# Agents innermost in `signed_weights`, with the second sets written by ScalarE and by the eviction

## The chip, the cores and the metric

The kernel is a Bass and Tile program on one core of one Trainium2 chip. The metric is the device time of one execution in microseconds, on that core, as the median of several runs. Engines are named as in the profile: PE (TensorE matmul), PEld (TensorE weight load), DVE (VectorE), ACT (ScalarE), POOL (GpSimd) and SP (the engine that issues DMAs).

## The reference, cut to what matters

```python
# attention through 49 agents: B, N, C = 4, 10048, 128
a2k = sm(agents, k)                 # softmax of scale * agents @ k.T
agent_v = a2k @ v                   # 49 x 128 per batch
x = (sm(q, agents) @ agent_v).reshape(B * N, C)
# mixture of experts: 4 groups of 4 experts, F = 1024
g_idx = argmax(x @ w_group, 1)                  # and its softmax weight g_w
e_idx = argmax(x @ w_expert[g_idx], 1)          # and its softmax weight e_w
out = g_w * e_w * (relu(x @ w1[g, e]) @ w2[g, e])   # one expert for each row
```

Each row of x is a convex mixture of 49 agent rows of its batch. So for one expert, x @ w1 is a mixture of the 49 rows of agent_v @ w1, and a hidden unit whose 49 entries all have one sign is linear (or zero) for every row.

## The kernel before, in words

The four batches run in the order 1, 2, 0, 3 of the input, called batch 0 to 3 here. For each batch there is work of four sorts: keys and values to agent_v (`agents_of`), queries to the softmax rows and the routing (`queries_of`, `routing`, `output_weight`), the weights of the batch's most frequent expert (`weights_in`), and the tiles of that expert (`tiles`): per tile of 512 rows three units of `first` (products with the small weights into a PSUM bank `ph`, eviction `hh` by ACT, remainder `hl` by DVE) and `second` (into `po`), and three `check` products into `pv`, whose largest violation ACT gathers (`spare`). `second` runs three units behind `first` (LAG = 3). Rows of the third batch that go to other experts are done by `taken`, which prepares the weights of two more experts (`prepare_kept`).

**What sets the order.** All of this is written as generators, six streams (m tiles, a agents, q queries, w weights, s stores, g gathers). Everything for batch 0 up to its weights stands in a hand-written list (ORDER); after that the string PLAN has one letter for a step of a stream (z is one idle matmul that nobody reads), and each `yield` ends a step. Every engine runs its instructions in exactly that program order. So an instruction put on another engine takes the place, in that engine's queue, at which its step stands in PLAN.

**The edited function.** `signed_weights` makes one expert's weights for `first`, and runs six times: for batch 0, 1, 2, for two kept experts, for batch 3. These are calls 1 to 6. Its stages:

- Ordering. Eight matmuls (w1f as weights, the 49 agents moving) give the coefficients, `ps`, 128 x (8 blocks of hidden units x 49 agents). ACT evicts them as `mt` (fp32) and `mh` (fp16, in the trace mth). On DVE: the sum `ss` and the sign s16 of each hidden unit, `ms` = mh times the sign, the deviation `dv` (it lives in the tile of ml), times `peak` and its minimum; the square of mt and its sum; a key for each unit; `below` and `cntf` count keys under 32 levels; two PE products and a scan give each unit a position `pos`. `peak` is a bound for each agent of a batch, made in `peaks` (three times, for batches 1 to 3) and used here.
- One-hots. `hot` (8 comparisons of 512 positions on DVE) sorts the hidden units by position.
- Second copies. The weight operand of a product has 98 columns, the 49 agents twice, since `first` multiplies by 49 high parts and 49 low parts. So mh, ml = mt - mh (mtl), mt and mv (mtv) each have two equal sets of 49.
- Products on PE, all reading the one-hots: mh and ml (8 each, 384 columns), `whl` (24, 256 columns: w2 sorted, its high and low part), mt with w2f (8 products in fp32, two records each in the trace, for what lies beyond the first 384 positions), mv with `hot` (8, 128 columns), and then mv with a second set of one-hots (8, 512 columns).

Before, each of the four tiles is laid out as [P, 2, NA, FB]: set, agent, block, with the block innermost. `twice` takes all 98 columns of one block, so it reads every eighth element. The PSUM bank has the block outermost, so its evictions and the reductions over agents (`rearrange("p a k -> p k a")`) step by eight elements too. The second set is in every case a DVE `tensor_copy`, right behind what makes the first.

**PSUM.** Pool `psa` has five banks with one tag, "at". All of the products above, the transposes of `turn`, the units `ph` and the checks `pv` take their bank there in program order. `ps2` has two banks for `po`, and one bank is for the idle matmuls. Tiles of pool `rt` (mt, mth, mtl, mtv, hot, ...) have one buffer.

Of the kernel before, what the change touches and what calls it, by code (L numbers as in the profile page):

```python
# [10 lines left out]
F32 = mybir.dt.float32  # L11
F16 = mybir.dt.float16
# [3 lines left out]
AF = mybir.ActivationFunctionType  # L16
ALU = mybir.AluOpType
AX = mybir.AxisListType
# [4 lines left out]
P = 128  # L23
# [3 lines left out]
NA = 49  # L27
# [3 lines left out]
FB = F // P  # L31
# [169 lines left out]
def build(ctx, tc, qT, kT, v, agT, wr, w1, w2, cpk, out):  # L201
    nc = tc.nc
    pe, vec, act, pool, sync = [Pinned(x) for x in (nc.tensor, nc.vector, nc.scalar, nc.gpsimd, nc.sync)]
# [6 lines left out]
    const = ctx.enter_context(tc.tile_pool(name="const", bufs=1))  # L210
# [3 lines left out]
    rt = ctx.enter_context(tc.tile_pool(name="rt", bufs=1))  # L214
# [9 lines left out]
    def bank(b=1):  # L224

        if alone[0] and b == 0:
            turns[0] += 1
            k = turns[0] % 8
            if k in (1, 4):
                return ps2.tile([P, TQ, C], F32, name="po").rearrange("p a c -> p (a c)")  # L230
        return psa.tile([P, 512], F32, name="at", tag="at")
# [5 lines left out]
    def cc(name):  # L237
        o, w = CCOL[name]
        return cp[:, o:o + w]
# [11 lines left out]
    pool.memset(flags, 0.0)  # L251
    within = const.tile([P, 2, MOSTH + 1], F32, name="within")
    pool.memset(within, 0.0)
    peak = const.tile([P, NA, FB], F16, name="peak")
    pool.memset(peak, 0.25)
    two = const.tile([P, NA], F32, name="two")
    vec.tensor_add(out=two, in0=identf[:, 0:NA], in1=identf[:, HALF:HALF + NA])
# [198 lines left out]
    def agents_of(b):  # L456

        state[b] = {}
        st = state[b]
        n = len(chunks)  # L460
        yield from skewed(n, lambda ci: load_only("k", b, ci), lambda ci: key_load(b, ci), lambda ci: key_scores(b, ci))
        yield from key_max(b)
        yield from skewed(n, lambda ci: value_load(b, ci), lambda ci: value_exp(b, ci), lambda ci: value_products(b, ci))
        acc = st["acc"]
        sides = [slice(x, x + NA) for x in (0, HALF)]
        av = rt.tile([P, C + 1], F32, name="av2")
        pool.memset(av[HALF // 2:HALF], 0.0)
        act.activation(av[sides[0]], acc[sides[0], 0:C + 1], AF.Copy)
        yield FINE
        vec.tensor_copy(out=av[sides[1]], in_=acc[sides[1], 0:C + 1])  # L470
        yield
        ps = bank(b)
        both = slice(0, SIDES)
        pe.matmul(ps[:, 0:NA], av[both, C:C + 1].broadcast_to([SIDES, P]), two[both], start=True, stop=True)
        pe.matmul(ps[:, NA:2 * NA], av[both, 0:C], two[both], start=True, stop=True)
        yield
        za = sm.tile([P, NA], F32, name="za2")
        vec.tensor_scalar(out=za, in0=ps[:, 0:NA], scalar1=1e-9, scalar2=None, op0=ALU.add)
        vec.reciprocal(out=za, in_=za)
        avT = sm.tile([P, NA], F32, name="avT")  # L480
        vec.tensor_mul(out=avT, in0=ps[:, NA:2 * NA], in1=za)
        yield
        yield from agents_scaled(b, avT)

    def front(b, early, order, later):
# [34 lines left out]
        for x in order:  # L520
# [87 lines left out]
            elif o == "J":  # L608
                parted["q", b, c] = split_load("q", b, c)
            elif o == "z":  # L610
                busy(c)
            elif o == "i":
                busy(c, psT[:, 384:512])
            elif o == "A":
                psT = main_soon(b, early, a0, se, busy)
                alone[0] = False
            elif o == "D":
                scaled = scaled or coarse(agents_scaled(b, psT[:, 0:NA]))
                for _ in range(c):
                    next(scaled, None)  # L620
            elif o == "U":
                uf = early.tile([P, P], F32, name="uf")
                pin(sync.dma_start(out=uf, in_=cpk[:, CUSED:CUSED + P]))
                pool.tensor_copy(out=upper, in_=uf)
            elif o == "W":
                weights = signed_weights(b, wbuf[b % 2], state[b].pop("wf"))
                counted = coarse(weights)
                for _ in range(c):
                    next(counted)
                pinned(())  # L630
            elif o == "F":
                all_of(logits_of(b, 0))
            elif o == "R":
                all_of(routing(b, *RANGES[0]))
            elif o == "n":
                for _ in range(c):
                    next(later)
# [395 lines left out]
    def peaks(b):  # L1033

        st = state[b]
        pm = rt.tile([P, NT, NA], F16, name="pm", tag="hot")
        for i in range(0, NT, 20):
            t = slice(i, min(i + 20, NT))
            vec.tensor_mul(out=pm[:, t], in0=rows[:, t, 0:NA], in1=st["inv"][:, t].unsqueeze(2).broadcast_to([P, t.stop - i, NA]))
            yield  # L1040
        vec.tensor_max(out=pm[:, 0:39], in0=pm[:, 0:39], in1=pm[:, 40:79])
        yield FINE
        for n in (20, 10, 5):
            vec.tensor_max(out=pm[:, 0:n], in0=pm[:, 0:n], in1=pm[:, n:2 * n])
        px = sm.tile([P, NA], F32, name="px")
        vec.tensor_reduce(out=px, in_=pm[:, 0:5].rearrange("p t a -> p a t"), axis=AX.X, op=ALU.max)
        yield
        ps = bank(b)
        pe.transpose(ps[0:NA, 0:P], px, identf)
        yield  # L1050
        ma = sm.tile([NA, 1], F32, name="ma")
        vec.tensor_reduce(out=ma, in_=ps[0:NA, 0:P], axis=AX.X, op=ALU.max)
        yield
        ps = bank(b)
        pe.matmul(ps[:, 0:NA], ma.broadcast_to([NA, P]), identf[0:NA, 0:NA], start=True, stop=True)
        yield
        vec.tensor_copy(out=peak, in_=ps[:, 0:NA].unsqueeze(2).broadcast_to([P, NA, FB]))
        yield

    def signed_weights(b, to, wf):  # L1060
# [2 lines left out]
        w1f, w2f = wf  # L1063
        wb = to.bitcast(F16)
        f32 = lambda n, name: rt.tile([P, n], F32, name=name)
        of_k = lambda a: a.unsqueeze(1).broadcast_to([P, NA, FB])
        twice = lambda a, k: a.rearrange("p i a k -> p (i a) k")[:, :, k]
        ps = bank(b)
        for k in range(FB):
            pe.matmul(ps[:, k * NA:(k + 1) * NA], w1f[:, k * P:(k + 1) * P], st["at"][:, 0:NA], start=True, stop=True)  # L1070
        yield
        psk = ps[:, 0:FB * NA].rearrange("p (k a) -> p k a", a=NA)
        psa_ = psk.rearrange("p k a -> p a k")
        mt2 = rt.tile([P, 2, NA, FB], F32, name="mt")
        mh2, ml2, mv2 = [rt.tile([P, 2, NA, FB], F16, name=name) for name in ("mth", "mtl", "mtv")]
        mt, mh, ml, mv = [x[:, 0] for x in (mt2, mh2, ml2, mv2)]
        act.activation(mt, psa_, AF.Copy)
        yield FINE
        act.activation(mh, psa_, AF.Copy)
        yield FINE  # L1080
        ss, qq, mu, mn, va, key, pl, sg = [f32(FB, "f" + name) for name in ("ss", "qq", "mu", "mn", "va", "key", "pl", "sg")]
        vec.tensor_reduce(out=ss, in_=psk, axis=AX.X, op=ALU.add)
# [6 lines left out]
        vec.scalar_tensor_tensor(out=mu, in0=ss, scalar=1.0 / NA, in1=s16, op0=ALU.mult, op1=ALU.mult)  # L1089
        yield  # L1090
        dv = ml
        sq = rt.tile([P, NA, FB], F32, name="sq", tag="big")
        ms = mv
        vec.tensor_mul(out=ms, in0=mh, in1=of_k(s16))
        yield FINE
        vec.tensor_sub(out=dv, in0=ms, in1=of_k(mu))
        yield FINE
        vec.tensor_mul(out=dv, in0=dv, in1=peak)
        yield FINE
        vec.tensor_reduce(out=mn, in_=dv.rearrange("p a k -> p k a"), axis=AX.X, op=ALU.min)  # L1100
        yield
        vec.tensor_mul(out=sq, in0=mt, in1=mt)
        yield FINE
        vec.tensor_reduce(out=qq, in_=sq.rearrange("p a k -> p k a"), axis=AX.X, op=ALU.add)
        yield FINE
        vec.tensor_add(out=mn, in0=mn, in1=mu)
        yield FINE
# [16 lines left out]
                          in1=cc("level").unsqueeze(2).broadcast_to([P, MOSTH, FB]), op=ALU.is_lt)  # L1124
        yield FINE
        cnt = rt.tile([P, MOSTH], F16, name="cntf")
        with nc.allow_low_precision("counts of at most 8"):
            vec.tensor_reduce(out=cnt, in_=below, axis=AX.X, op=ALU.add)
        yield
        ps = bank(b)  # L1130
# [4 lines left out]
                          in1=cc("most").unsqueeze(2).broadcast_to([P, 2, MOSTH]), op=ALU.is_le)  # L1135
# [6 lines left out]
                       in1=sel.unsqueeze(2).broadcast_to([P, 2, 2, MOSTH]))  # L1142
# [33 lines left out]
        for k in range(FB):  # L1176
            vec.tensor_scalar(out=hot[:, k], in0=wide, scalar1=pos[:, k:k + 1], scalar2=None, op0=ALU.is_equal)
            if k % 4 == 3:
                yield
        vec.tensor_copy(out=mh2[:, 1], in_=mh)  # L1180
        yield FINE
        vec.tensor_sub(out=ml, in0=mt, in1=mh)
        yield FINE
        vec.tensor_copy(out=ml2[:, 1], in_=ml)
        yield FINE
        whl = rt.tile([P, FB, 2, C], F16, name="whl", tag="big")
        act.activation(whl[:, :, 0], w2f, AF.Copy, scale=W2S)
# [3 lines left out]
        for src, to_ in ((mh2, 0), (ml2, WLO)):  # L1191
            ps = bank(b)
# [5 lines left out]
        yield FINE  # L1198
        vec.tensor_mul(out=mt, in0=mt, in1=of_k(sg))
        yield FINE  # L1200
        vec.tensor_copy(out=mt2[:, 1], in_=mt)
        yield FINE
        vec.tensor_reduce(out=qq, in_=mh.rearrange("p a k -> p k a"), axis=AX.X, op=ALU.max, apply_absolute_value=True)
        yield FINE
        vec.tensor_scalar(out=qq, in0=qq, scalar1=2.0 ** -9, scalar2=2.0 ** -23, op0=ALU.mult, op1=ALU.add)
        yield FINE
        vec.tensor_sub(out=mv, in0=ms, in1=of_k(qq))
        yield FINE
        vec.tensor_copy(out=mv2[:, 1], in_=mv)
        yield  # L1210
        for j0 in range(0, FULL, 2):
            n = min(2, FULL - j0)
            ps = bank(b)
# [6 lines left out]
        ps = bank(b)  # L1220
# [9 lines left out]
        for h, (f0, f1) in enumerate(((EX, TS), (0, TS))):  # L1230
# [6 lines left out]
            ps = bank(b)  # L1237
# [20 lines left out]
    def weights_in(b):  # L1258

        yield from output_weight(b)  # L1260
        yield from peaks(b)
        yield from signed_weights(b, wbuf[b % 2], state[b].pop("wf"))
# [560 lines left out]
    def one_by_one(*gens):  # L1823

        for gen in gens:
            yield from gen
            yield "end"
# [4 lines left out]
        a=one_by_one(*[agents_of(b) for b in later_ones]),  # L1832
# [35 lines left out]
```

## Time and profile before

| | |
|---|---|
| median of 3 runs | 816.7 us (815.06 to 817.57) |
| the profiled execution: its time | 810.57 us |
| its span | 808.8 us |
| granted TensorE clock, mean | 0.975 |
| PE busy | 744.7 us, 92% |
| PEld busy | 559.9 us, 69% |
| DVE busy | 644.3 us, 80% |
| ACT busy | 502.3 us, 62% |
| POOL busy | 379.3 us, 47% |
| SP | issues DMAs only, not counted as busy |

The span is from the first to the last record of the profile; the execution's time has 1.8 us more. PEld runs beside PE, so their times overlap. One helper records every operation, so all rows of the trace name one line, L185; the tile names (out<-in) tell what an instruction is.

### The profile page before, as it was taken

The page shows a single profiled execution, that of the slowest core. Times are in us where ns is not written, and L with a number is a line of the kernel's source. Part 1 is how long each engine was busy: PE and PEld are TensorE (multiplying, and loading weights), DVE is VectorE, ACT ScalarE, POOL GpSimd, SP SyncE. Part 2 cuts the span into 40 slices and gives each one's busy share as a digit, 9 for nine tenths or more (in the row PEclk, how much of TensorE's full clock was granted, in tenths as well). Part 3 has the DMA queues.
Part 4 walks back from the last instruction along what each step waited for, and adds up shares of the span by engine and source line. Part 5 has one row for each costly group of instructions (what it writes and reads, how often), then busy time and mean ns, then how long its engine had stood idle before and what let it go on. Part 6 is the DMA issues. An engine that isn't in the chain of part 4 may idle for free.

```text
span 808.8 us, 23174 instructions
## 1 busy us (share of the span) xinstructions
PE 744.7 (92%) x9350; PEld 559.9 (69%) x9350; DVE 644.3 (80%) x1455; ACT 502.3 (62%) x1075; POOL 379.3 (47%) x619
## 2 busy tenths in 40 slices
PE   7888999999998899999979998899999998999994
PEld 6664767767765577888647755677787675977773
DVE  6869978976889886777997899958968987876663
ACT  5543577759955444899555323447988775457772
POOL 4235574129941521688385216843663226542220
PEclk9979999999999999999998999999999998999997
DMA  9844143497623737443366040175402373112211
GB/s 321 318 158 156 38 147 118 122 319 205 178 67 142 230 100 248 123 136 94 98 253 191 7 156 18 16 210 152 147 15 71 109 247 88 58 43 63 67 54 53
DMA packets 66276, 107.93 MB, mean 133 GB/s; under 512 B 5223, under 2 KB 46136, under 8 KB 65776
## 3 DMA queue, kind: packets, MB, share of 16 engines
q1 hardware_dynamic: 64816, 104.54, 40.1%
q0 software_dynamic: 1344, 1.82, 1.0%
q8 instruction: 75, 1.23, 0.6%
q14 instruction: 41, 0.34, 0.2%
HBM read 73.97 MB, written 32.47 MB: 132 GB/s over the span
## 4 chain that ended last, share of the span: by engine, by line
PE 52%; DVE 21%; ACT 5%; issue 3%; DMA 2%; POOL 1%; another core or an unknown queue 1%; SPq 0%; ACTq 0%; POOLq 0%; DVEq 0%
PE po L185 17%; PE at L185 17%; PE ph L185 10%; PE pv L185 5%; DVE hl L185 4%; PE idle L185 3%; DVE pm L185 2%; DMA vf<-v 1%; DVE oh L185 1%; ACT hh L185 1%; ACT xh L185 1%; DMA w1f<-w 1%; DVE rd L185 1%; DVE rx L185 1%; POOL xl L185 1%
## 5 line engine op out<-in xcount | busy, mean ns | idle before, releaser
L185 POOL TENSOR_TENSOR xl<-xf,xh 128x256 f16<-128x256 f32 (+2 forms) x280 | 194.0, 725 | 147.7 <-ACT xh L185 134.3
L185 DVE SCALAR_TENSOR_TENSOR hl<-ph,hh 128x512 f16<-128x512 f32 (+1 forms) x256 | 172.8, 678 | 75.1 <-ACT hh L185 70.9
L185 PE MATMUL po<-wbuf,hh 128*128 128x128 f16 x1896 | 185.2, 219 | 0.3 <-issue 0.3
L185 ACT ACTIVATE hh<-ph 128x512 f16<-128x512 f32 (+1 forms) x256 | 151.4, 592 | 53.5 <-PE ph L185 47.7
L185 PEld LDWEIGHTS <-hh 128*128 128x128 f16 x2022 | 161.2, 98 | 32.1 <-issue 1.1
L185 PE MATMUL po<-wbuf,hl 128*128 128x128 f16 x948 | 171.2, 219 | 0.0
L185 PE MATMUL ph<-et,wbuf 98*128 98x512 f16 x480 | 141.9, 377 | 9.9 <-DVE hl L185 4.6
L185 ACT ACTIVATE spare<-pv 128x512 bf16<-128x512 f32 (+1 forms) x158 | 93.4, 591 | 81.1 <-PE pv L185 73.8
L185 PE MATMUL idle<-wide,ident 128*128 128x512 f16 x515 | 143.0, 388 | 0.0
L185 POOL TENSOR_TENSOR oo<-oo,cw 128x256 f32<-128x256 f32 x116 | 72.9, 648 | 142.4 <-ACT oo L185 124.7
L185 PEld LDWEIGHTS <-hl 128*128 128x128 f16 x1011 | 99.0, 98 | 0.4 <-issue 0.4
L185 PEld LDWEIGHTS <-wbuf 98*128 98x128 f16 x720 | 61.5, 98 | 49.3 <-issue 18.9
L185 PE MATMUL pv<-et,wbuf 98*128 98x512 f16 x240 | 91.0, 379 | 1.2 <-ACT lg L185 0.6
L185 PEld LDWEIGHTS <-ident 128*128 128x128 f16 x653 | 57.5, 103 | 45.6 <-issue 5.4
L185 ACT ACTIVATE xh<-xf 128x1024 f16<-128x1024 f32 (+2 forms) x78 | 81.4, 1047 | 11.0 <-DMA xf<-kT 8.0
L185 PEld LDWEIGHTS <-et 98*128 98x128 f16 x1264 | 62.6, 97 | 22.1 <-issue 0.9
L185 POOL TENSOR_TENSOR rows<-ef,rows 128x147 f16<-128x147 f32 (+1 forms) x108 | 44.0, 435 | 63.9 <-ACT rows L185 62.2
L185 PEld LDWEIGHTS <-xh 128*128 128x128 f16 (+1 forms) x1264 | 60.7, 97 | 15.8 <-issue 3.3
L185 DVE TENSOR_REDUCE flags<-pv 128x1 f32<-128x512 f32 x98 | 66.7, 681 | 5.1 <-PE pv L185 2.6
L185 PE MATMUL at<-agh,xl 128*128 128x49 f16 (+1 forms) x545 | 53.5, 185 | 1.8 <-POOL xl L185 1.6
L185 PE MATMUL at<-agh,xh 128*128 128x49 f16 (+1 forms) x545 | 53.7, 186 | 0.0
L185 PEld LDWEIGHTS <-xl 128*128 128x128 f16 (+1 forms) x632 | 50.8, 96 | 3.7 <-POOL xl L185 2.5
(375 smaller groups left out, 1350.8 us busy)
## 6 DMA issues: line engine op xcount, KB each, us to landing
xf<-qT SPq DMA_DIRECT2D x38, 512.0 KB, 5.2
out<-oo SPq DMA_DIRECT2D x76, 256.0 KB, 4.0
vf<-v SPq DMA_DIRECT2D x36, 516.0 KB, 5.6
xf<-kT SPq DMA_DIRECT2D x35, 512.0 KB, 4.8
erow<-rows SPq DMA_DIRECT2D x3, 1975.0 KB, 7.7
wsl<-wkept SPq DMA_DIRECT2D x6, 544.0 KB, 4.2
w2f<-w SPq DMA_DIRECT2D x6, 512.0 KB, 6.8
w1f<-w SPq DMA_DIRECT2D x5, 512.0 KB, 5.4
```

The source lines that it names most:

```text
L185: y = f(*a, **k)
```

## The change

The four tiles become [P, FB, 2, NA]: block, set, agent, so that the 98 columns of one block adjoin and so do the 49 elements that a reduction takes. The evictions read the bank in its own order. The mh eviction writes both sets at once, reading the bank through a broadcast; its DVE copy goes, but its step stays. The second sets of ml, mt and mv are copied by ACT, not DVE, in the same steps. Factors of one value per block (sign, mean, margin: `of_k`) are broadcast along the innermost axis now. `peak` keeps 49 values and is broadcast over blocks where it is used. PLAN and ORDER stay letter by letter, and so does the number of steps.

```diff
@@ -251,7 +251,7 @@
     pool.memset(flags, 0.0)
     within = const.tile([P, 2, MOSTH + 1], F32, name="within")
     pool.memset(within, 0.0)
-    peak = const.tile([P, NA, FB], F16, name="peak")
+    peak = const.tile([P, NA], F16, name="peak")
     pool.memset(peak, 0.25)
     two = const.tile([P, NA], F32, name="two")
     vec.tensor_add(out=two, in0=identf[:, 0:NA], in1=identf[:, HALF:HALF + NA])
@@ -1054,7 +1054,7 @@
         ps = bank(b)
         pe.matmul(ps[:, 0:NA], ma.broadcast_to([NA, P]), identf[0:NA, 0:NA], start=True, stop=True)
         yield
-        vec.tensor_copy(out=peak, in_=ps[:, 0:NA].unsqueeze(2).broadcast_to([P, NA, FB]))
+        vec.tensor_copy(out=peak, in_=ps[:, 0:NA])
         yield
 
     def signed_weights(b, to, wf):
@@ -1063,20 +1063,19 @@
         w1f, w2f = wf
         wb = to.bitcast(F16)
         f32 = lambda n, name: rt.tile([P, n], F32, name=name)
-        of_k = lambda a: a.unsqueeze(1).broadcast_to([P, NA, FB])
-        twice = lambda a, k: a.rearrange("p i a k -> p (i a) k")[:, :, k]
+        of_k = lambda a: a.unsqueeze(2).broadcast_to([P, FB, NA])
+        twice = lambda a, k: a[:, k].rearrange("p i a -> p (i a)")
         ps = bank(b)
         for k in range(FB):
             pe.matmul(ps[:, k * NA:(k + 1) * NA], w1f[:, k * P:(k + 1) * P], st["at"][:, 0:NA], start=True, stop=True)
         yield
         psk = ps[:, 0:FB * NA].rearrange("p (k a) -> p k a", a=NA)
-        psa_ = psk.rearrange("p k a -> p a k")
-        mt2 = rt.tile([P, 2, NA, FB], F32, name="mt")
-        mh2, ml2, mv2 = [rt.tile([P, 2, NA, FB], F16, name=name) for name in ("mth", "mtl", "mtv")]
-        mt, mh, ml, mv = [x[:, 0] for x in (mt2, mh2, ml2, mv2)]
-        act.activation(mt, psa_, AF.Copy)
-        yield FINE
-        act.activation(mh, psa_, AF.Copy)
+        mt2 = rt.tile([P, FB, 2, NA], F32, name="mt")
+        mh2, ml2, mv2 = [rt.tile([P, FB, 2, NA], F16, name=name) for name in ("mth", "mtl", "mtv")]
+        mt, mh, ml, mv = [x[:, :, 0] for x in (mt2, mh2, ml2, mv2)]
+        act.activation(mt, psk, AF.Copy)
+        yield FINE
+        act.activation(mh2, psk.unsqueeze(2).broadcast_to([P, FB, 2, NA]), AF.Copy)
         yield FINE
         ss, qq, mu, mn, va, key, pl, sg = [f32(FB, "f" + name) for name in ("ss", "qq", "mu", "mn", "va", "key", "pl", "sg")]
         vec.tensor_reduce(out=ss, in_=psk, axis=AX.X, op=ALU.add)
@@ -1089,19 +1088,19 @@
         vec.scalar_tensor_tensor(out=mu, in0=ss, scalar=1.0 / NA, in1=s16, op0=ALU.mult, op1=ALU.mult)
         yield
         dv = ml
-        sq = rt.tile([P, NA, FB], F32, name="sq", tag="big")
+        sq = rt.tile([P, FB, NA], F32, name="sq", tag="big")
         ms = mv
         vec.tensor_mul(out=ms, in0=mh, in1=of_k(s16))
         yield FINE
         vec.tensor_sub(out=dv, in0=ms, in1=of_k(mu))
         yield FINE
-        vec.tensor_mul(out=dv, in0=dv, in1=peak)
-        yield FINE
-        vec.tensor_reduce(out=mn, in_=dv.rearrange("p a k -> p k a"), axis=AX.X, op=ALU.min)
+        vec.tensor_mul(out=dv, in0=dv, in1=peak.unsqueeze(1).broadcast_to([P, FB, NA]))
+        yield FINE
+        vec.tensor_reduce(out=mn, in_=dv, axis=AX.X, op=ALU.min)
         yield
         vec.tensor_mul(out=sq, in0=mt, in1=mt)
         yield FINE
-        vec.tensor_reduce(out=qq, in_=sq.rearrange("p a k -> p k a"), axis=AX.X, op=ALU.add)
+        vec.tensor_reduce(out=qq, in_=sq, axis=AX.X, op=ALU.add)
         yield FINE
         vec.tensor_add(out=mn, in0=mn, in1=mu)
         yield FINE
@@ -1177,11 +1176,10 @@
             vec.tensor_scalar(out=hot[:, k], in0=wide, scalar1=pos[:, k:k + 1], scalar2=None, op0=ALU.is_equal)
             if k % 4 == 3:
                 yield
-        vec.tensor_copy(out=mh2[:, 1], in_=mh)
         yield FINE
         vec.tensor_sub(out=ml, in0=mt, in1=mh)
         yield FINE
-        vec.tensor_copy(out=ml2[:, 1], in_=ml)
+        act.activation(ml2[:, :, 1], ml, AF.Copy)
         yield FINE
         whl = rt.tile([P, FB, 2, C], F16, name="whl", tag="big")
         act.activation(whl[:, :, 0], w2f, AF.Copy, scale=W2S)
@@ -1198,15 +1196,15 @@
         yield FINE
         vec.tensor_mul(out=mt, in0=mt, in1=of_k(sg))
         yield FINE
-        vec.tensor_copy(out=mt2[:, 1], in_=mt)
-        yield FINE
-        vec.tensor_reduce(out=qq, in_=mh.rearrange("p a k -> p k a"), axis=AX.X, op=ALU.max, apply_absolute_value=True)
+        act.activation(mt2[:, :, 1], mt, AF.Copy)
+        yield FINE
+        vec.tensor_reduce(out=qq, in_=mh, axis=AX.X, op=ALU.max, apply_absolute_value=True)
         yield FINE
         vec.tensor_scalar(out=qq, in0=qq, scalar1=2.0 ** -9, scalar2=2.0 ** -23, op0=ALU.mult, op1=ALU.add)
         yield FINE
         vec.tensor_sub(out=mv, in0=ms, in1=of_k(qq))
         yield FINE
-        vec.tensor_copy(out=mv2[:, 1], in_=mv)
+        act.activation(mv2[:, :, 1], mv, AF.Copy)
         yield
         for j0 in range(0, FULL, 2):
             n = min(2, FULL - j0)
```

## Rows read from the trace of the kernel before

**Rows 1.** Chain of work that ended last, shares of the span by engine

```profile
PE 52%; DVE 21%; ACT 5%; issue 3%; DMA 2%; POOL 1%; another core or an unknown queue 1%; SPq 0%; ACTq 0%; POOLq 0%; DVEq 0%
```

**Rows 2.** Timeline of PE, call 6: start, duration, instruction, count, idle before

```profile
692.78 1.58 PE L185 MATMUL at<-hot,mth 128*98 128x384 f16 x8
...
697.37 2.79 PE L185 MATMUL at<-whl,hot 128*128 128x256 f16 x24
...
699.99 3.09 PE L185 MATMUL at<-w2f,mt 128*98 128x128 f32 x16
...
702.92 1.55 PE L185 MATMUL at<-hot,mtv 128*98 128x128 f16 x8
```

**Rows 3.** Lines by form, weight loads: busy us, mean ns, idle before, releaser

```profile
L185 PEld LDWEIGHTS <-rows 128*98 128x98 f16 x316 | 23.2, 128 | 3.0 <-DVE ef L185 0.4 <-issue 0.2
...
L185 PEld LDWEIGHTS <-mtv 128*98 128x98 f16 x96 | 20.1, 264 | 1.8 <-issue 1.1
...
L185 PEld LDWEIGHTS at<-w2f,mt 128*98 128x98 f32 x96 | 18.1, 278 | 0.2
```

**Rows 4.** Timeline of PEld, eight loads of softmax rows

```profile
131.58 0.52 PEld L185 LDWEIGHTS <-rows 128*98 128x98 f16 x8
```

**Rows 5.** Timeline of PE, the coefficients of call 2

```profile
264.06 1.99 PE L185 MATMUL at<-at,w1f 128*128 128x49 f32 x16 [0.26 <-DMA w1f<-w]
```

**Rows 6.** One tile, mth: ns min/median/max, first and last start

```profile
L185 DVE TENSOR_TENSOR mtv<-mth,s x6: 354/356/903, 62.2 to 666.4; 128x392 f16<-128x392 f16 x6
...
L185 DVE COPY mth<-mth x6: 250/310/666, 81.8 to 691.5; 128x392 f16<-128x392 f16 x6
...
L185 DVE TENSOR_REDUCE fqq<-mth x6: 843/850/881, 86.8 to 698.3; 128x8 f32<-128x392 f16 x6
```

**Rows 7.** Lines by form, DVE

```profile
L185 DVE TENSOR_TENSOR pm<-rows,inv 128x980 f16<-128x980 f16 x9 | 12.4, 1422 | 0.0
...
L185 DVE TENSOR_REDUCE fss<-at 128x8 f32<-128x392 f32 x6 | 3.4, 566 | 7.5 <-ACT mth L185 6.2 <-PE pv L185 1.2
...
L185 DVE COPY mt<-mt 128x392 f32<-128x392 f32 x6 | 2.7, 449 | 0.2
```

**Rows 8.** Lines by form, ACT

```profile
L185 ACT ACTIVATE hh<-ph 128x512 f16<-128x512 f32 x243 | 145.1, 597 | 51.2 <-PE ph L185 45.5 <-DVE flags L185 3.8 <-issue 0.8
...
L185 ACT ACTIVATE rows<-ef 128x392 f16<-128x392 f32 x35 | 19.1, 545 | 0.6
...
L185 ACT ACTIVATE mth<-at 128x392 f16<-128x392 f32 x6 | 3.0, 492 | 0.0
```

**Rows 9.** Timeline of ACT, near the mtl subtractions of calls 1, 3, 4, 6

```profile
76.06 0.50 ACT L185 ACTIVATE S<-at 128x392 f32<-128x392 f32 x1 [0.22 <-PE at L185]
...
442.36 0.60 ACT L185 ACTIVATE oo<-po 128x512 f32<-128x512 f32 x1
...
446.27 0.90 ACT L185 ACTIVATE xh<-xf 128x832 f16<-128x832 f32 x1
...
515.80 0.59 ACT L185 ACTIVATE hh<-ph 128x512 f16<-128x512 f32 x1
...
688.31 0.60 ACT L185 ACTIVATE spare<-pv 128x512 bf16<-128x512 f32 x1 [0.69 <-PE ph L185]
```

**Rows 10.** Timeline of DVE, mtl subtractions of calls 1, 3, 4, 6

```profile
82.00 0.56 DVE L185 TENSOR_TENSOR mtl<-mt,mth 128x392 f16<-128x392 f32 x1
...
447.78 0.56 DVE L185 TENSOR_TENSOR mtl<-mt,mth 128x392 f16<-128x392 f32 x1
...
517.91 0.55 DVE L185 TENSOR_TENSOR mtl<-mt,mth 128x392 f16<-128x392 f32 x1
...
691.87 0.55 DVE L185 TENSOR_TENSOR mtl<-mt,mth 128x392 f16<-128x392 f32 x1
```

**Rows 11.** Timeline of PE, mth of call 3 and a unit of call 6

```profile
447.92 1.76 PE L185 MATMUL at<-hot,mth 128*98 128x384 f16 x8 [1.07 <-DVE mth L185]
...
691.46 0.59 PE L185 MATMUL ph<-ets,wsl 98*128 98x512 f16 x2
```

## Prediction

> **What bounds the kernel now.** I read the chain of work that ended last first. PE holds 52% of it, DVE 21%, ACT 5% [rows 1]: time taken from PE, or put in front of it, counts nearly in full; time on ACT counts where PE or DVE then waits. Next I looked at what the edited function does in time. It runs six times (four batches and two kept experts, at about 59, 265, 428, 499, 540 to 600 and 664 us; "calls 1 to 6"). Each run has an ordering stretch, almost all DVE, and a product stretch, almost all PE: 8 matmuls with mth, 8 with mtl, 24 with whl, 16 records of fp32 with mt, 8 and 8 with mtv. In call 6 they stand back to back on PE [rows 2].
>
> **Part 1: the weight loads.** As weights, mt, mth, mtl and mtv are read every eighth element now and adjoining after. The spacing of n matmuls is (whole stretch minus the last one's own duration) over n-1. For mth that is (1.58-0.34)/7 = 0.18 us, for mt (3.09-0.35)/15 = 0.18, for the 128-column mtv (1.55-0.34)/7 = 0.17 to 0.18, though their moving columns differ: 384, fp32 128 and 128 [rows 2]. So the load sets the pace: one takes 264 to 278 ns, one of 98 adjoining columns 128 ns [rows 3], and those follow each other at (0.52-0.13)/7 = 0.056 us [rows 4]. The 256-column whl matmuls run at (2.79-0.27)/23 = 0.109 us, which is one column in 0.43 ns [rows 2]; so 384 columns want 0.16 us. New paces: mth and mtl 0.16 (saves 16 x 0.02 = 0.32 us a call), first mtv 0.056 (8 x 0.124 = 0.99), second mtv, 512 columns, none. For fp32 the nearest row is w1f, fp32 weights of 128 adjoining columns, at (1.99-0.2)/15 = 0.12 us [rows 5]; I take 0.11 for mt, since 98 columns are fewer: 16 x 0.073 = 1.17. Below: nothing for mt, if its fp32 moving columns hold it at 0.18. Sum 2.48 us a call, 1.31 at the least.
>
> The Trainium skill, "TensorE: Matmul & The Clock Gate", section "LDWEIGHTS", gives a load its columns over 1.2 in ns, by estimate 82 ns for 98 columns. By that the first mtv would save 0.78 a call and not 0.99; the measured 0.056 us disagrees and decides.
>
> **Part 2: DVE.** Four copies go: mth's takes 0.31 us in the median [rows 6], mt's 0.45 in the mean [rows 7], the others about as mth's, so 1.4 us a call. Three reductions lose their stride: 0.85 us each now [rows 6], against 0.57 for as many elements read in order [rows 7], so 3 x 0.28 = 0.85. The multiply by the sign gets worse. Now both fp16 operands run in order and it takes 0.36 in the median [rows 6]; after, one sign stands for 49 elements, as in pm<-rows,inv: 1.42 us for 980, or 0.57 for 392 [rows 7]. That adds 0.21 (0 if the fp16 pace stays). The peak eviction shrinks from 392 elements to 49, some 0.35 us in three calls.
>
> Only some of this is on the path. The ordering stretch holds two of the three reductions (-0.56), the multiply (+0.2) and waits for the mth eviction, which now writes twice as much: the slope from 392 to 512 elements is (597-492)/120 = 0.875 ns, so 784 cost 0.84 and not 0.49, +0.34 [rows 8]. Where DVE waits for that eviction (calls 1 to 3) the stretch gains nothing. In calls 4 and 6, where DVE is late anyway, it gains 0.4 each: -0.8. The mth copy's 0.25 to 0.67 us lies just ahead of the first product; it is inside the walk below.
>
> **Part 3: three copies on ACT, and what queues behind them.** One costs about 0.54 us (the cast of 392 elements from SBUF, [rows 8]); 3 x 0.54 + 0.34 = 2.0 us a call, 12 in all, which ACT has spare. The wait is dearer. The mtl copy needs DVE's mtl subtraction, which comes after eight hot comparisons; ACT now runs ahead of DVE there, and after cannot. Its place on ACT follows from the code: hh and hl of one step are issued side by side, and copy and hl stand in a known order on DVE.
>
> Call 6: ACT ends a spare at 688.9, DVE's subtraction ends at 692.4 [rows 9, 10], 0.4 sooner without the mth copy. ACT stands still for 3.1 us and then owes hh, spare, hh, ets, spare, hh, all of which ran in that gap; the last ends near 695.7, not 692.9. PSUM feels it: pool psa has five banks for all of at, ph and pv. At 691.46 [rows 11] ph wants one; by then three ph wait for hl, and two pv and one er transpose for ACT. The first bank comes free at 693.7, so PE is 2.25 late there and, with mth and mtl themselves shorter, 1.9 at the end of whl; mt and mtv then give back 2.15. Net -0.25.
>
> Call 3: ACT ends oo at 442.96, the subtraction ends at 448.34 [rows 9, 10], 448.08 without the copy. Behind it queue S, spare, whl, hh and xh. xh then starts near 451.2 and not 446.27 [rows 9]; four POOL subtractions, the scores and the next products wait for it. The bank for mth comes at 448.8, not 447.66, so the 1.07 that PE waits for DVE now [rows 11] does not shrink. The whl products end 3.1 late; mt and mtv give back 2.1: net +1.0.
>
> The same walk for the others, starting for calls 1 and 4 from ACT free at 76.56 and 516.39 and the subtraction ending at 82.56 and 518.46 [rows 9, 10]; calls 2 and 5 lie between these in what ACT owes:
>
> Late at the end of the whl products, given back after, net: call 1: 1.0, 0, +1.0 (2 us late on DVE, half lost in PE's fillers); call 2: 2.4, 1.3, +1.1 (the mtv copy waits too, ahead of an eviction that holds a bank); call 3: 3.1, 2.1, +1.0; call 4: 0.8, 1.9, -1.1; call 5: 1.5, 2.2, -0.7; call 6: 1.9, 2.15, -0.25. Sum 10.7 late, 9.65 given back, +1.05. With the -0.8 of Part 2: +0.25 us.
>
> **Against which time.** The profiled execution took 810.57 us, 808.8 of span and 1.8 around it; the runs' median is 816.7 (815.06 to 817.57), 6.1 above. I add the sum to the median: 817.0 us. A change under 0.3%, 2.45 us here, can't be told from none.
>
> **Rivals.**
>
> A, faster: ACT's wait doesn't reach PE. For it: PE works three steps behind (LAG), and ACT is idle often enough to catch up. Against: five banks are full in calls 2, 3 and 6 at the critical moment. With none of the 10.7 arriving, and all five late calls keeping 2.48, it is 816.7 - 12.4 - 0.8 = 803.5; with half arriving, 811.6. It decides from 2.7 us of the 10.7 left out.
> The Trainium skill, "TensorE: Matmul & The Clock Gate", section "Architectural detail: the array is 16x 32x32, not 1x 128x128", calls ACT's and DVE's queues strictly first in, first out: no later eviction passes a waiting copy. The trace agrees as far as it goes: its ACT records stand in program order throughout. Could they pass, A would be the forecast.
>
> B, slower: the gains of mt and mtv don't come, because those matmuls then wait for mt2 and mtv2, made late on ACT. Place: the 24 whl products must outlast the mt chain on DVE and ACT. For it: in call 2 the mtv copy waits for a late subtraction, in a queue that the mtl wait has already delayed. Against: in call 6 the whl products cover 2.6 us [rows 2]. All gains lost: 816.7 + 10.7 - 0.8 = 826.6; half lost: 821.8. It decides from 2.2 us lost.
>
> C, the loads stay at their pace: 826.6 as in B, but 128 ns for 98 adjoining columns speaks against it [rows 3]; 0.03, counted in B.
>
> **Chances.** Two sums near ten that nearly cancel, each known to a few us: within 0.3% 0.38; A 0.31; B with C 0.31. The forecast's own range is 814.5 to 819.5. Taking in half-way A (811.6) and half-way B (821.8) with a margin, and leaving out a tenth on each side, 809.5 to 824.
>
> **What would show it.** Right: loads of mtv at about 128 ns, spaced 0.056; mt records spaced 0.11; reductions at 0.57; ACT idle before each mtl copy for 1.6 to 6 us, ended by DVE mtl; PE waiting for ACT or a bank just ahead of mth in calls 2, 3 and 6; product stretches 2 us shorter. Wrong: mt records still at 0.18; ACT copies without idle time before them; PE unbroken ahead of mth.

## The result, and the profile after

The change is slower: 822.68 us (821.57 to 825.16) against 817.13 us for the kernel before (815.06 to 818.45), a ratio of 1.0067, 95% interval 1.0044 to 1.0089. That is 5.5 us and more than the 2.45 us that can be told from no change. The range of 809.5 to 824.0 holds it; the likeliest case, within 0.3%, did not come. It ended on the slower side, which had 0.31. The profiled execution took 822.23 us with a span of 820.4.

PE's share of the chain that ended last fell from 52% [rows 1] to 46%, and ACT's rose from 5% to 7%. The page, part 4:

```profile
PE 46%; DVE 24%; ACT 7%; issue 3%; DMA 2%; POOL 1%; another core or an unknown queue 1%; SPq 0%; DVEq 0%; ACTq 0%; POOLq 0%
```

The weight loads got their speed. In call 6 the products stand back to back as in [rows 2]; here is the timeline of PE after the change:

```profile
711.24 2.79 PE L185 MATMUL at<-whl,hot 128*128 128x256 f16 x24
713.86 1.91 PE L185 MATMUL at<-w2f,mt 128*98 128x128 f32 x16
715.61 0.61 PE L185 MATMUL at<-hot,mtv 128*98 128x128 f16 x8
```

The unedited whl products take 2.79 us as before. The mt records went from 3.09 to 1.91 us, the first mtv products from 1.55 to 0.61. Start to start, the median spacing of mt records is 0.109 us (forecast 0.11), that of the first mtv 0.056 (0.056), that of mth and mtl 0.162 (0.16). The loads themselves, by form, to be set beside [rows 3]:

```profile
L185 PEld LDWEIGHTS at<-w2f,mt 128*98 128x98 f32 x96 | 12.4, 185 | 2.6 <-ACT wbuf L185 2.4
L185 PEld LDWEIGHTS <-mtv 128*98 128x98 f16 x96 | 9.4, 123 | 8.9 <-issue 4.5
```

On DVE the reductions came out at 0.55 us (forecast 0.57) and the multiply by the sign at 0.65 on average, 0.2 more than before, and at 0.56 in the median (forecast 0.57). The square of mt was not expected to move; it rose from 0.61 to 0.79 us on average. The rise is in calls 1 to 3 alone (1.01 to 1.07 us; 0.55 to 0.56 in calls 4 to 6), and why stays open. The lines of DVE, by form:

```profile
L185 DVE TENSOR_TENSOR sq<-mt 128x392 f32<-128x392 f32 x6 | 4.8, 794 | 0.0
...
L185 DVE TENSOR_TENSOR mtv<-mth,s 128x392 f16<-128x392 f16 x6 | 3.9, 652 | 0.0
...
L185 DVE TENSOR_REDUCE fqq<-mth 128x8 f32<-128x392 f16 x6 | 3.3, 550 | 0.0
```

And ACT, by form. The last column is the idle time just before the group and what ended it:

```profile
L185 ACT ACTIVATE mth<-at 128x784 f16<-128x784 f32 x6 | 4.9, 815 | 0.0
...
L185 ACT ACTIVATE mt<-mt 128x392 f32<-128x392 f32 x6 | 3.2, 532 | 4.3 <-DVE mt L185 4.3
L185 ACT ACTIVATE mtl<-mtl 128x392 f16<-128x392 f16 x6 | 3.2, 532 | 21.1 <-DVE mtl L185 17.2 <-issue 3.9
L185 ACT ACTIVATE mtv<-mtv 128x392 f16<-128x392 f16 x6 | 3.2, 530 | 4.8 <-DVE mtv L185 4.0 <-DVE fqq L185 0.7
```

A copy costs 0.53 us (forecast 0.54), the eviction of both sets 0.815 (0.84). Ahead of the six mtl copies ACT stands idle for 21.1 us in all: 4.34, 4.34, 5.28, 1.22, 2.01 and 3.89 in calls 1 to 6.

**Where the time went.** Both traces have the same 9350 matmuls in the same order, so each can be matched with itself. The lag of one is its start after the change minus its start before. The lag, in us, at the first and last matmul of the stages of each call, before against the change:

```
call   first w1f   first mth   last whl   first mt   last mt   last mtv   first w1f of the next call
1        -0.6        -1.2        -0.1       -0.1       -1.1       0.4       -0.5
2        -0.5         5.0         5.7        7.3        7.8       8.0        6.2
3         6.2         7.4        11.0       11.0        9.9       9.0        9.0
4         9.0         9.9         9.9        9.9        8.8       9.2        9.2
5         9.2         8.4        10.5       10.0        8.8       8.0        8.3
6         8.3        14.0        13.9       13.9       12.8      11.8       11.9 (end)
```

The lag adds up to 11.9 us, since this execution of the kernel before was a quick one (810.57 against a median near 817). The last call loses 5.7 us up to its first mth and gives 2.2 back, but two executions of the kernel before differ as much there, as a later section shows. One call stands out: call 2 loses 8.0 us from the place where both are level again (283.7 us, lag 0.0) to its last mtv. The prediction had 1.1 there. The timeline of ACT in call 2 after the change shows the start of it:

```profile
281.82 0.89 ACT L185 ACTIVATE xh<-xf 128x832 f16<-128x832 f32 x1
287.05 0.53 ACT L185 ACTIVATE mtl<-mtl 128x392 f16<-128x392 f16 x1 [4.34 <-DVE mtl L185]
287.49 0.58 ACT L185 ACTIVATE spare<-pv 128x512 bf16<-128x512 f32 x1
...
301.43 0.53 ACT L185 ACTIVATE mtv<-mtv 128x392 f16<-128x392 f16 x1 [1.88 <-DVE mtv L185]
301.87 0.58 ACT L185 ACTIVATE wbuf<-at 128x512 f16<-128x512 f32 x1
```

From 282.7 ACT waits for DVE, and everything queued behind the mtl copy waits too, the first being the `spare` eviction that frees a PSUM bank. It happens again with the mtv copy, which ACT waits for until 301.4; behind that stands the eviction of the whl products. PE meanwhile, in its own timeline:

```profile
284.85 0.38 PE L185 MATMUL idle<-wide,ident 128*128 128x512 f16 x1
288.21 0.80 PE L185 MATMUL ph<-et,wbuf 98*128 98x384 f16 x2 [2.98 <-ACT spare L185]
...
291.08 1.46 PE L185 MATMUL idle<-wide,ident 128*128 128x512 f16 x3
...
302.50 3.73 PE L185 MATMUL at<-w2f,mt 128*98 128x128 f32 x16 [2.19 <-ACT wbuf L185]
```

PE has no bank for ph until `spare` has run (2.98 us idle), and no bank for the mt products until the whl eviction has (2.19). Behind each wait it is also slow: three idle matmuls of 512 columns start (1.46-0.63)/2 = 0.41 us apart here (0.63 is the duration of the last), against 0.22 in the same place before, and the 16 mt records take 3.73 us, twice the 1.91 of call 6. The table by stretches (busy times, then the granted clock PEclk, DMA share, GB/s) says why:

```profile
284.00:288.00 4.00, 1.23 (x31) 0.88 (x29) 3.62 (x10) 0.95 (x3) 1.08 (x2) 0.92 0.01 4
288.00:293.00 5.00, 4.79 (x30) 3.16 (x30) 2.32 (x4) 2.92 (x9) 0.00 (x0) 0.50 0.83 263
293.00:300.00 7.00, 5.98 (x41) 4.47 (x40) 2.54 (x5) 2.85 (x6) 2.11 (x3) 0.91 0.01 3
300.00:303.00 3.00, 0.79 (x3) 0.62 (x4) 1.47 (x4) 1.57 (x4) 0.77 (x2) 0.67 0.00 0
303.00:308.00 5.00, 5.00 (x22) 3.88 (x21) 1.71 (x5) 0.67 (x3) 0.00 (x0) 0.51 0.12 20
308.00:312.00 4.00, 4.00 (x80) 3.63 (x80) 3.27 (x9) 3.02 (x9) 1.49 (x3) 1.00 0.53 162
```

The granted clock fell to 0.50, the lower of its two levels (1.2 and not 2.4 GHz), and the table shows 5 us behind each wait at 0.50 and 0.51; behind the first wait about 1.3 us of the next stretch (0.91 of 7 us) were slow too. In the kernel before it stood at 1.00 through the same stretches. By these two stretches half of 5 us is lost twice, by estimate about 2.5 us each. The lag agrees: it was 3.1 us when PE started again at 288.2 and 5.7 at 293.9, and it grew from 7.3 us at the first mt to 8.6 at 307.9, though mt's shorter loads should have taken 1.2 off. The Trainium skill, "TensorE: Matmul & The Clock Gate", section "Terms", prices a throttled stretch in the same way, at its length times one minus the ratio of the clocks. The 2.6 us by which the first lag grew agree with that.

### The profile page after: what moved, and what is told of

It reads as the page before. It is cut to its first block, busy times and chain, and to the rows that moved or that the text cites. A ratio compares the mean times of both kernels' runs of the same rounds, so it can differ in the third digit from the quotient of the medians.

```text
span 820.4 us, 23160 instructions
## 1 busy us (share of the span) xinstructions
PE 739.4 (90%) x9350; PEld 541.0 (66%) x9350; DVE 633.2 (77%) x1431; ACT 509.8 (62%) x1093; POOL 376.6 (46%) x619
## 4 chain that ended last, share of the span: by engine, by line
PE 46%; DVE 24%; ACT 7%; issue 3%; DMA 2%; POOL 1%; another core or an unknown queue 1%; SPq 0%; DVEq 0%; ACTq 0%; POOLq 0%
PE po L185 16%; PE at L185 14%; PE ph L185 9%; PE pv L185 4%; DVE hl L185 4%; PE idle L185 3%; DVE pm L185 2%; DVE hot L185 2%; ACT hh L185 2%; DVE oh L185 1%; ACT xh L185 1%; DMA w1f<-w 1%; DVE rd L185 1%; DMA xf<-qT 1%
```

## The experiments

The wait theory says: ACT takes its instructions in order; a copy that waits for DVE holds back the evictions behind it, PE runs out of banks, idles, and pays again at the lower clock. The rivals were the new layout itself (layout theory: DVE's broadcasts, the longer mh eviction) and ACT's added work as such (work theory). The kernel before took 804 to 814 us on the chips of these runs and 817 on that of the prediction, so all of it is told in ratios, each against the kernel before on the same chip; the expectations in us were reckoned from 817.

**All three copies on DVE, layout kept.**

```diff
-        act.activation(ml2[:, :, 1], ml, AF.Copy)
+        vec.tensor_copy(out=ml2[:, :, 1], in_=ml)
...
-        act.activation(mt2[:, :, 1], mt, AF.Copy)
+        vec.tensor_copy(out=mt2[:, :, 1], in_=mt)
...
-        act.activation(mv2[:, :, 1], mv, AF.Copy)
+        vec.tensor_copy(out=mv2[:, :, 1], in_=mv)
```

> The new layout and the mh eviction of both sets stay; the second sets of ml, mt and mv are copied by DVE again. Wait theory (ACT's copies stand in its queue waiting for DVE, evictions behind them hold the PSUM banks, PE stalls and its granted clock falls): all of the loss goes and the shorter weight loads stay, some 1.3 to 2.5 us in each of six calls less about 1 us of DVE copies: 804 to 810 us, faster than before. Layout theory (DVE's broadcasts along the innermost axis and the longer mh eviction cost it): 820 to 824 us, as the change. Work theory (it is ACT's 1.6 us of copying in each call, not the wait): 806 to 812; the run without the wait tells it from the first.

796.39 us against 804.9, ratio 0.9893 (0.9878 to 0.9908). Layout theory is out: the layout makes the kernel faster. The ratio is inside the expectation of the wait theory (804 to 810 of 817 is 0.984 to 0.991), and of the work theory.

**Only the ml copy on DVE** (the first of the three pairs of lines above).

> Only the ml copy goes back to DVE; mt and mv are still copied by ACT. Wait theory: the 21.1 us that ACT stands idle ahead of the six mtl copies go, the stalls behind the mt and mv copies (about 2 us of PE idle in call 2, and the low clock after it) stay: 807 to 813 us. Layout theory: 820 to 824. Work theory: a third of the copying goes, so a third of the way from the change to the kernel with all copies on DVE: 816 to 819.

800.82 us, ratio 0.9949 (0.9928 to 0.997), at the upper bound of the wait theory (813 of 817 is 0.995). Of the 1.0067 of the change 0.0118, 9.5 us, go with the mtl copy alone, far more than a third of the way. The mt and mtv copies on ACT cost the remaining 0.0056, 4.4 us.

**The same work on ACT without the wait.**

```diff
-        act.activation(ml2[:, :, 1], ml, AF.Copy)
+        act.activation(ml2[:, :, 1], mh2[:, :, 0], AF.Copy)
```

> ACT still copies 392 elements into the second set of ml, at the same place of its queue, but from the first set of mh, which ACT itself wrote long before; so it does the same work and waits for nothing (the low parts of the weights of the second agent set are then those of mh). Wait theory: as with the ml copy on DVE, 806 to 813 us. Work theory: as the change, 820 to 824.

798.29 us, ratio 0.9916 (0.99 to 0.9933). Its line among ACT's groups, by form:

```profile
L185 ACT ACTIVATE mtl<-mth 128x392 f16<-128x392 f16 x6 | 3.2, 531 | 0.0
```

The same 3.2 us of copying with nothing idle ahead, and the mtl copy's loss is gone (the expectation of 806 to 813 is 0.987 to 0.995). Work theory is out.

**The wait without the work.** On the kernel with three DVE copies:

```diff
         vec.tensor_copy(out=ml2[:, :, 1], in_=ml)
+        unread = rt.tile([P, 1], F16, name="unread")
+        act.activation(unread, ml[:, 0, 0:1], AF.Copy)
```

> The kernel with all three copies on DVE, and at the place where the change has ACT copy ml, ACT reads one element of each partition of it into a tile that nobody uses: the wait without the work. Wait theory: most of what the ml copy costs on ACT comes back, ratio 0.999 to 1.004, against 0.989 without it. Work theory: 0.989 to 0.992.

809.93 us against 803.91, ratio 1.0075 (1.0047 to 1.0102): above what the wait theory expected, and as slow as the change. By form:

```profile
L185 ACT ACTIVATE unread<-mtl 128x1 f16<-128x1 f16 x6 | 1.2, 206 | 25.8 <-DVE mtl L185 25.8
```

Six instructions of 0.2 us, which wait 25.8 us in all, cost 0.0182, 14.6 us, over the kernel without them. That is more than the 0.0118 that went with the mtl copy above, so the parts do not simply add up; why stays open. It is not all in call 2 either: matched with the kernel before on the same chip, the lag grows there by 2.4 us from 283.6 us to the last mtv (2.1 to 4.4), and by 8.0 in the change.

**The old layout with the three copies on ACT.** The kernel before, with

```diff
-        vec.tensor_copy(out=ml2[:, 1], in_=ml)
+        act.activation(ml2[:, 1], ml, AF.Copy)
...
-        vec.tensor_copy(out=mt2[:, 1], in_=mt)
+        act.activation(mt2[:, 1], mt, AF.Copy)
...
-        vec.tensor_copy(out=mv2[:, 1], in_=mv)
+        act.activation(mv2[:, 1], mv, AF.Copy)
```

> The kernel before, with its layout, and only the second sets of ml, mt and mv copied by ACT in the same steps. Wait theory: all of the loss and none of the shorter loads: 826 to 836 us, above the change. Layout theory: 814 to 819, as before.

823.66 us against 804.9, ratio 1.0239 (1.0217 to 1.0262). The wait theory's 826 to 836 is 1.011 to 1.023 of 817; the loss is at or a little above its upper bound. By form, ACT waits 26.3 us ahead of the mtl copies, and the loads of mtv keep their 264 ns:

```profile
L185 ACT ACTIVATE mtl<-mtl 128x392 f16<-128x392 f16 x6 | 3.2, 529 | 26.3 <-DVE mtl L185 26.3
...
L185 PEld LDWEIGHTS <-mtv 128*98 128x98 f16 x96 | 20.1, 264 | 1.4 <-issue 0.6
```

**The change again, the layout alone, and two other places.** These four ran on one chip.

> The change itself once more, for its time against the kernel before on one chip with the three below. Every theory: its ratio as measured, 1.004 to 1.009.

811.01 us against 804.52, ratio 1.0078 (1.0049 to 1.0108).

The layout alone, with mh's second set by DVE too:

```diff
-        act.activation(mh2, psk.unsqueeze(2).broadcast_to([P, FB, 2, NA]), AF.Copy)
+        act.activation(mh, psk, AF.Copy)
...
+        vec.tensor_copy(out=mh2[:, :, 1], in_=mh)
```

> The new layout alone: each second set is copied by DVE, that of mh too, and the eviction of mh writes one set. Wait theory with the layout as the whole gain: as the kernel with all three copies on DVE, ratio 0.988 to 0.991, since 0.3 us of DVE ahead of the products against 0.33 us less of eviction ahead of the ordering nearly cancel. If the eviction of both sets is worth its six DVE copies in full (6 x 0.31 = 1.9 us, 0.23%): 0.9916. If the doubled eviction costs (0.33 us in each ordering stretch, 2 us): 0.987.

796.88 us, ratio 0.9904 (0.9871 to 0.9937), the same as with the eviction of both sets. Whether that eviction is worth anything can't be told: the interval holds the first two cases and ends beside the third (0.9871 against 0.987).

The change with one line moved three steps on:

```diff
-        act.activation(ml2[:, :, 1], ml, AF.Copy)
...
+        act.activation(ml2[:, :, 1], ml, AF.Copy)
         for src, to_ in ((mh2, 0), (ml2, WLO)):
             ps = bank(b)
```

> The change with one line moved: ACT copies the second set of ml three steps later, at the head of the step that issues the mh products, behind the cast to whl and whatever stands between. Wait theory: the wait is short there, and what stands behind it is the mh eviction, which waits for PE anyway; so near the run without the wait, ratio 0.990 to 0.996. Work theory (ACT's added work, wherever it stands): 1.004 to 1.009, as the change.

797.63 us, ratio 0.9919 (0.9891 to 0.9946), 1.6% below the change. By form:

```profile
L185 ACT ACTIVATE mtl<-mtl 128x392 f16<-128x392 f16 x6 | 3.2, 541 | 6.1 <-DVE mtl L185 6.1
```

The wait shrank from 25.0 us on this chip to 6.1, and what is left stands ahead of an eviction that waits for PE anyway. The rule that the prediction's rival A cited, from the Trainium skill, "TensorE: Matmul & The Clock Gate", section "Architectural detail: the array is 16x 32x32, not 1x 128x128", that ACT's queue is strictly first in, first out, agrees with this run: where one waiting instruction stands in the queue is all that differs from the change, and the 1.6% go with it.

That place for ml, and mt and mv copied by DVE:

> New layout, mh by one eviction, ml copied by ACT at the later place, mt and mv copied by DVE. If only waits cost and DVE's copies ahead of the products cost their 0.25 us each: 0.3 to 0.4% below the kernel with all copies on DVE, ratio 0.985 to 0.988. If the later place still holds evictions back: 0.990 to 0.995.

795.83 us, ratio 0.9897 (0.9864 to 0.9931). Neither expectation is singled out. It can't be told from the kernel with three DVE copies (0.9893), so ml on ACT at the late place is worth nothing measurable, with the 6.5 us in all that it still waits there. These two and the layout alone are the best kernels here.

**The kernel before against itself**, for its trace:

> The kernel before against itself, for its trace on this chip. Every theory: ratio 1.000.

Ratio 1.0005 (0.9986 to 1.0024). The lag of the repeated change against this execution confirms call 2: 0.9 at 283.6 us, 8.9 at its last mtv, 8.0 lost. In the other calls it is -0.2 (call 1), -0.3, -2.2, 1.6 and -0.1 (3 to 6, from the first w1f of a call to the next one's or the end). Only call 2 repeats in both pairs with the same size. The two executions of the kernel before, matched with each other, show how much of this is chance: from one call's first w1f to the next one's they differ by up to 3.0 us in calls 1 to 5 and by 7.3 us in call 6, but by only 0.6 us over the stretch in which call 2 loses its 8.0.

**What the clock costs.** The change with 24 more idle matmuls ahead of the two waits of call 2:

```diff
-    for x in PLAN:
+    for x in PLAN[0:1407] + 14 * "z" + PLAN[1407:1436] + 10 * "z" + PLAN[1436:]:
```

> The change with 24 idle matmuls more, 14 ahead of the ph products that wait 3.2 us for a bank in call 2 and 10 ahead of the mt products that wait 2.2 us there; each takes about 0.215 us at the full clock, so they fill the waits. If the lower granted clock behind these two waits costs what the lag of the trace grows by at it (some 2 to 3 us and 2 us): 4 to 5 us faster than the change, ratio 1.001 to 1.004. If the clock costs nothing, or falls anyway: 1.007 to 1.011.

807.21 us against 803.91, ratio 1.0042 (1.0022 to 1.0061). In the table by stretches the clock holds:

```profile
290.00:294.00 4.00, 3.78 (x36) 2.54 (x35) 2.59 (x5) 3.46 (x10) 0.00 (x0) 1.00 0.66 187
...
303.00:308.00 5.00, 4.95 (x62) 4.10 (x60) 3.59 (x10) 2.05 (x5) 0.00 (x0) 1.00 0.38 109
```

PE waits as long as before for its banks (the ph products start at 290.86 behind 15 idle matmuls that take 3.40 us) but goes on at full clock. From 283.6 us of the kernel before to the last mtv of call 2 the lag grows by 2.7 us (from 3.6 to 6.3), against 8.0 for the change: 5.3 gained, a little above what was expected. The timed ratios differ by 0.0036, 2.9 us, below it, and their intervals (1.0022 to 1.0061, and 1.0049 to 1.0108) overlap a little. So the clock's part is shown in the trace, and its size in the whole lies at some 3 to 5 us.

**Call 2 alone.** The change, with DVE copies where `b == 1`:

```diff
+        if b == 1:
+            vec.tensor_copy(out=ml2[:, :, 1], in_=ml)
+        else:
+            act.activation(ml2[:, :, 1], ml, AF.Copy)
```

(and mt, mv in the same way)

> The change, but in call 2 alone DVE copies the second sets of ml, mt and mv; ACT does in the other five calls. If call 2 carries the loss, as the lag of PE in the traces says (8 us there in both pairs): all of that goes, ratio 0.995 to 0.999. If the loss is spread evenly over the calls that wait (as the prediction's walk had it, 1.1 of some 4 us): 1.004 to 1.006.

810.66 us against 814.26, ratio 0.9969 (0.9952 to 0.9985). Call 2's three copies are worth 0.0098 to 0.0109, some 8 to 9 us: without them the change would have been a gain. The other five calls cost the 0.0076 that are left to the kernel with all copies on DVE, 6 us.

## Why the prediction was right and wrong, by its steps

**Part 1 was right for the loads.** The paces came out to within 0.003 us. What a call gets back from mt and mtv shows in the lag between first mt and last mtv of calls 3 and 6: 2.0 and 2.1 us, forecast 2.1. The whole kernel keeps less of it. The prediction's rival A had 12.4 + 0.8 = 13.2 us for a change whose waits reach nobody; the kernels without the waits gain 7.7 to 8.6 (ratios 0.9904 and 0.9893; they still pay DVE's copies). One place where it goes is seen: after call 4 PE in that kernel waits 3.44 us for the value load, a DMA, which the trace of the kernel before has no wait for in its place. One row of PE's timeline, with all copies on DVE:

```profile
537.00 1.39 PE L185 MATMUL at<-vf,S 128*49 128x129 f32 x13 [3.44 <-DMA vf<-v]
```

**Part 2 was right where it was priced.** The gain of 0.8 us in the ordering of calls 4 and 6 can't be separated in the lag from what differs between executions.

**Part 3 had the mechanism right and its size wrong, and that is the failed step.** It named the copy, what it waits for, the queue behind it and the PSUM banks, and it had ACT idle for 1.6 to 6 us ahead of each copy, where 1.2 to 5.3 were found. The walk failed at "calls 2 and 5 lie between these in what ACT owes". Call 5 came out near it in the first pair of traces (forecast -0.7, measured 9.2 to 8.3), though not in the second (1.6). Call 2 did not: forecast 2.4 late and 1.3 given back, net 1.1; measured 5.7 late at the end of whl, nothing given back, and 2.4 more lost, net 8.0. Three things make the difference. PE's wait for the bank, 3.0 to 3.2 us, is longer than the 2.4. The granted clock falls to 0.50 behind it; no term of the sum and no rival had the clock, though it nearly doubled the price of this wait (3.1 us of lag before it, 5.7 behind). And the mtv copy's wait, which the walk for call 2 named, made a second wait of PE, 2.19 us ahead of mt, with a second stretch at 0.50 in which mt's shorter loads were worth nothing.

**The two sums.** Forecast: 10.7 us late against 9.65 given back and 0.8 of ordering. Measured, from ratios: 14.9 us for the three copies on ACT (1.0078 less 0.9893, of 804.5) against 8.6 gained without their waits. Both were wrong by a few us, the cost too small and the gain too large; the difference, 6.3 us, is that of the change. Rival A failed since the waits do reach PE. Rival B had the right sign, the right call and the mtv copy, but not the right link: mt's products did not wait for mt2; they waited for a bank that an eviction behind the mtv copy would free. That the range holds the result is luck in part: both errors went the same way, and the upper end had been drawn with room for half of rival B (821.8), a link that did not come.

## What to carry to other kernels

A copy moved to an engine that runs ahead cost its wait here and not its work: six instructions of 0.2 us cost 14.6 us in all, and the same copy three steps later cost nothing that could be measured. Before moving an instruction to an in-order engine, find when its operand is made, what that engine has done by then, and which PSUM banks the instructions behind it hold. Where such a wait leaves PE idle, look at the granted clock behind it, and price the stretch at the lower level too.

## What the runs showed of the hardware that was not expected

The granted clock fell to 0.50 after PE idled 2.98 us, in a stretch that was otherwise dense, and stayed there for 6 us of work (288.2 to 294.2 us); in the repeated change it did so after 3.24 us and again after waits of 1.05 and 2.18 us that only one 0.28 us record divides, but in the same execution not after the single waits of 2.00 us (call 3) and 2.44 us (call 6), behind which the clock of the next 2 us was 1.00. The length of the wait alone does not tell which it will be: the same wait of 2.51 us, for `cntf` in call 2, was followed by 2 us at 0.50 in the trace of the change (277.2 us) and by 2 us at 1.00 in that of the repeated change (278.0). Idle matmuls in the two waits of call 2 kept it at 1.00.
